# Written order on all queues, eight pairs by seven products, and whole rows of scores, in a packed attention with a gated MLP

## The chip, the cores and the metric

The kernel runs on one core of a Trainium2 chip. The metric is the device time of one execution in microseconds; three runs of the kernel before gave 707.8, 708.59 and 708.6 us, median 708.59. The profile is of one more execution, whose span from the first to the last instruction is 707.7 us.

The names of the engines are those of the profile: PE is TensorE's matmuls, PEld its weight loads, DVE is VectorE, ACT is ScalarE, POOL is GpSimd, SP is SyncE, whose queue issues nearly all DMAs.

## What is computed

```python
# q, k, v: 8 batches x 8 heads x 576 rows x 64;  p: 8 x 8 x 32 x 64;  fp32
def sm_attn(qq, kk, vv):
    s = scale * (qq @ kk.T)
    a = exp(s - max(s)); a = a / (sum(a) + 1e-9)
    return a @ vv
p_packed = sm_attn(p, k, v)               # 32 packed rows per head
out = sm_attn(q, p_packed, p_packed)      # 576 x 64 per head
x = out with the heads side by side       # 4608 x 512
h = x @ w_in                              # w_in 512 x 2048, float64 on input
g = h * clip(h + 3, 0, 6) / 6
return g @ w_out                          # w_out 2048 x 512, float64 on input
```

## The kernel before

**Stages.** The packed rows are multiplied with w_in first ("m", 256 x 2048 for a batch, 32 packed rows of 8 heads), so the first product of a batch is m against the second softmax a: 256 deep, in two groups g. The 2048 columns of w_in are 16 blocks f of 128. For each f, `first_product` (L929) makes h for some rows of the batch; `gate_into` (L940 on ACT, L941 on DVE) makes h * min(relu(h + 3), 6); `split` (L946 on ACT, L947 on DVE or POOL) writes that as a hi and a lo part in fp32r; and `product` (L969) multiplies them with w_out, which is kept as hi and lo too. Every product is therefore three matmuls: hi by hi, hi by lo, lo by hi.

**Rows.** A batch has 576 rows, 4 x 128 and a boundary of 64. They are done in two halves c of 2 x 128 rows. One half of each batch is wide: its first product also covers the 64 boundary rows (320 columns instead of 256), whose gated values `keep_edge` (L965, POOL) puts into `bnd`. The boundary rows of two batches make one block of 128 rows for the second product. Before the change, those of batches 0 and 1 and of 2 and 3 are multiplied plainly in batches 1 and 3 (`edge_parts`, `edge_product`); those of 4 to 7 are multiplied in one pass in batch 7 (`moe_edges`), with rows of batches 4 and 5 kept in DRAM meanwhile (`e_kept`).

**Seven products.** Two blocks f, two blocks of 128 rows and two halves of 256 output columns make a 2 x 2 by 2 x 2 product, which `pair_product` does with seven products of 256 columns instead of eight. The right factors are blocks of w_out and four combinations of them, T1 to T4; T3 takes a block's place, and T1, T2, T4 lie in tiles wt in the places of w_in's chunks 1 to 3. `combine` makes them once, in batch 1. The left factors are the gated blocks A11 to A22 and sums S1 to S4 (L1241, L1249, L1254 on DVE), split in tiles ge, gf and ga. The sums pile up in four PSUM banks A, B, C, D, and at the end of a half `pair_product` puts C and D together (L1134 on ACT, L1136 on POOL, L1139 on DVE) and `single_product` adds A and B (L1153) and stores the rows (L1156). PAIRS = 6 of the 8 pairs are done like this; the other four f are singles, plain products of 512 columns, at the end of each half. Batch 0 has all f plain, batch 1 its first half plain and 4 pairs in its second. Of the six pairs' T blocks four lie in SBUF at a time; `fetch_t` (L1105) brings pairs 0 or 4 and 1 or 5 back from DRAM (768 KB each), twice in each half.

**Attention of the next batch** runs beside the MLP of this one. Scores, in 32-column tiles of the array, come from `each_head` (L350) into PSUM, in the steady part half a row (288 columns) at a time, through banks that the accumulators leave free; e is transposed (L440), multiplied with v (L470), and the second scores and softmax follow. The quarters of m come from `u_m`, also L350, 512 columns each, with w_in's chunk fetched from DRAM into one place, w_in0 (1 MB each, L1428).

**What sets the order.** Batch 0 and the start of batch 1's attention are written out by hand: PLAN is a list of names, and each name takes one step of a generator; all of PE, DVE, ACT, POOL and SP follow that list. `ENGINES` says which engine does a step that several can do. From batch 1 on, the planner of the tile framework orders the instructions by its own estimates, within limits: `second` puts products one pair behind their first products, `behind_gates` holds the attention's steps behind gates, and STAGES, LATE, TURN and FETCHES say at which f which step may start.

**The start.** The inputs of batch 0 come in rows of four (1 KB runs) and a remainder of 64 rows by itself (`long_rows`, `rest_rows`, `load_rows`), so scores and transposes of batch 0 have a long and a short part (L678, L694, L720, L731, L803). Tiles of w_in and w_out, 512 KB in float64 each, are loaded in between and narrowed to fp32 by ACT, DVE and POOL (L199, L203).

Of the kernel before, what the change touches and what calls it, by code (L numbers as in the profile page):

```python
# [20 lines left out]


STAGES = (((0, 1), (6, 2), (19, 2)), ((0, 1), (10, 2), (19, 1)))


LATE = (3, 2, 1, 2, 1)
PAIRS = 6
FIRST_PAIRS = 4
TURN = (
    (5, 5, 6, 6, 7, 7, 7), (7, 8, 8, 9, 9, 9, 10), (10, 10, 11, 11, 12, 12, 12), (13, 13, 13, 14, 14, 15, 15),  # L30
    (27, 27, 28, 28, 28, 29, 29), (29, 29, 30, 30, 30, 31, 31),
)
FETCHES = (((5, 1), (7, 0)), ((5, 4), (7, 5)))

PLAN = """
in in in in lo0 lo2 in in k0 in p li0 k1 in p k0 k2 k1 kr k2 in s0 kr b2 s0 b0 k3 s0 b2 li1 s0 warm b2 s0 in
k3 b2 in b0 s1 s0 li2 q1 b2 e0 q1 c0 s1 b2 e0 q0 c0 li3 s0 s1 v0 q0 s0 s1 s1 v0 b0 lp s1 b0 e1 a0 v0 c1 qr
v0 e1 c1 s1 a0 z0 qr b0 s1 a0 z0 b0 v1 a0 z0a a1 z0a upper a1 z0a lo1 q2 v1 li4 a1 q3 q2 z0a a1 v1 q3 v1 z0a  # L40
z1 z1 li7 a2 m0 z1a a2 m1 a2 z1a a2 lo3 a3 z1b z0a lk0 a3 z1b z1b z0a z1b z0a z1a z0a z1b lo5 z1a b1 li6 z1a
z1b m0 z1b b1 z1a z1a z1b z0a a4 z1a m0 li5 z1b z0a warm a3 z1b z0a m1 m0 z1b a7 lk2 z1a h0 m0 z1a m1 b1 a7
z1a b1 b3 h0 b3 lo4 b3 a3 warm r0 m1 a4 r0 b3 m2 lo8 tp h1 r0 m1 a7 y0 b1 h1 r0 m2 lo6 a4 x0 b1 r1 a4 x0 m2
m2 a6 r1 x0 a6 m2 h2 a7 tk0 r1 h2 y1 a5 lk3 r1 a5 x0 y1 a5 x1 r2 a6 a5 b5 x1 r2 b3 x1 tk2 r2 y0 h3 a6 b4 r2
lk1 h3 b4 b5 m4 x1 b3 r3 b4 li8 b5 m4 b4 li10 r3 x2 li9 m4 m4 x2 lo7 r3 m4 b5 below h4 b4 tk3 y3 b6 h4 b4 y3
lq1 y2 b6 x2 r3 b5 x2 b6 r4 tk1 x3 b6 b8 r4 x3 a8 b5 S a8 x3 a8 r4 y4 a8 S S S S x3 b8 y4 h5 a10 li11 r4 a10
lo9 h5 a10 a9 b8 lq3 x4 b8 r5 x4 b6 r5 S x4 y2 a10 r5 tq1 h6 lo10 b8 r5 lq2 h6 y5 a9 y5 S x4 a9 r6 b8 x5 a9
S b7 S x5 r6 a11 x5 li12 S a11 a11 h7 b6 r6 a11 S h7 r6 x5 b9 r7 li13 m8 S lv b7 b7 x6 r7 y6 b7 m8 x6 y7 r7
m8 m8 x6 y6 S tq3 r7 b7 h8 S b10 m8 lq0 x6 b10 b7 y7 a12 h8 b10 b9 b9 x7 b10 tq2 r8 lo12 x7 S lw0 r8 x7 b9
a13 E h9 r8 S h9 y8 a13 a13 y8 lo11 r8 E a13 r9 x7 b10 x8 r9 E E tq0 b9 h10 a12 b9 lw1 E h10 S a12 y9 b12  # L50
b10 a12 x8 r10 x8 r9 li14 r10 E b12 x8 y9 li15 E r10 b12 h11 r9 b11 h11 r10 b11 b11 V r11 b11 x9 V V b12 b11
lo15 r11 T x9 a14 T a14 Z lo13 a14 b12 x9 a14 a15 Z a15 a15 x10 y11 Z a15 x9 b15 Z Z x10 r11 b11 m12 b15 x10
r11 b15 m12 b12 b15 x10 m12 m12 y10 x11 b13 m12 h12 Z y11 b15 lo14 y10 b13 Z h12 b13 x11 r12 b13 x11 Z r12
x11 Z r12 h13 b15 b14 h13 r12 b14 M b14 r13 x12 Z b14 b13 r13 Z x12 b14 Z r13 h14 Z y12 y12 h14 b13 x12 r13
r14 x12 Z r14 x13 Z r14 h15 Z y13 h15 y13 Z x13 b14 stage r15 x13 r14 y14 Z x13 r15 x14 Z r15 x14 y14 M Z
r15 x14 Z M M x15 Z x15 o0 Z x15 y15 o0 o1 M x14 Z o1 y15 x15 Z o3 o3 o2 o2
"""

ENGINES = {
# [16 lines left out]
def packed_attention_moe(  # L78
# [4 lines left out]
    v: bass.AP,  # L83
    p: bass.AP,
    w_in: bass.AP,
    w_out: bass.AP,
    out: bass.AP,
):

# [21 lines left out]
    scale = 1.0 / float(D) ** 0.5  # L111
    H2 = DM // 2
    W = 2 * P + REM
    WT = 2 * W

    const = ctx.enter_context(tc.tile_pool(name="const", bufs=1))
    mp = [ctx.enter_context(tc.tile_pool(name="mp", bufs=1))]
# [1407 lines left out]
```

## Time and profile before

| | before |
|---|---|
| median of three runs | 708.59 us (707.8 to 708.6) |
| span of the profiled execution | 707.7 us |
| PE: in flight | 684.7 us, 5924 matmuls |
| DVE busy | 544.2 us |
| ACT busy | 428.8 us |
| POOL busy | 335.9 us |
| DMA | 111 MB, 157 GB/s over the span |
| mean granted clock of TensorE | 0.990 of full speed |

Busy time of PE counts matmuls in flight, which overlap, so its share is no measure of pace. The distance between the starts of two matmuls is; the chain of waits in order of time shows it, since a run of matmuls that follow each other without a wait stands there as one piece with its length. Idle time stands beside the work that ended it.

### The profile page before, as it was taken

The numbers are of one execution on the slowest core, as the hardware profiler recorded it, in microseconds if no ns is written. First come the engines' busy times: TensorE is split into PE (matmuls) and PEld (weight loads), VectorE is DVE, ScalarE is ACT, GpSimd is POOL, SyncE is SP. The second block draws the span as 40 slices with busy tenths as digits, with TensorE's granted clock in tenths as the row PEclk, the third lists the DMA queues.
The fourth block names the chain that finished last, engine by engine and source line by source line (L and its number), as shares of the span: only waits on it lengthen the run. The fifth ranks groups of instructions, "written<-read, shape, count | busy, mean of one in ns | idle before, by whom it ended". The sixth has DMA issues, their size and how long they took to land.

```text
span 707.7 us, 16190 instructions
## 1 busy us (share of the span) xinstructions
PE 684.7 (97%) x5924; PEld 591.9 (84%) x5924; DVE 544.2 (77%) x1227; ACT 428.8 (61%) x1004; POOL 335.9 (47%) x515
## 2 busy tenths in 40 slices
PE   6599999999999999999999999999999999999997
PEld 4477877888879888899898888899888988899997
DVE  2897788788999759877788777877698778867754
ACT  5798876556566646565455655656475755565553
POOL 2475541113425456371272626474453646475552
PEclk9699999999999999999999999999999999999999
DMA  9989852955338655465554647375755644340330
GB/s 277 310 216 240 218 141 88 287 150 116 117 123 208 161 131 210 127 158 108 107 200 125 164 103 232 121 158 129 196 200 143 168 127 150 129 170 1 120 119 30
DMA packets 199679, 111.15 MB, mean 157 GB/s; under 512 B 173489, under 2 KB 185265, under 8 KB 195761
## 3 DMA queue, kind: packets, MB, share of 16 engines
q1 hardware_dynamic: 199056, 109.94, 55.8%
q8 instruction: 46, 0.75, 0.4%
q14 instruction: 33, 0.26, 0.1%
q10 hardware_dynamic: 544, 0.20, 0.1%
HBM read 92.27 MB, written 17.83 MB: 156 GB/s over the span
## 4 chain that ended last, share of the span: by engine, by line
PE 82%; DVE 7%; DMA 5%; issue 2%; SPq 1%; ACT 1%; POOL 1%; DVEq 0%; ACTq 0%; POOLq 0%
PE acc L969 48%; PE ps_hh L929 22%; PE ps L350 5%; PE ps_h L607 3%; DMA w_again<-w_kept 2%; PE ps L470 1%; SPq L294 1%; DMA room<-in_q_dram 1%; PE ps L440 1%; DMA wt<-t_kept 1%; DVE tr L555 1%; DMA p_nat<-in_p_dram 1%; DVE osb L1153 1%; PE ps L273 1%; DVE t L941 0%
## 5 line engine op out<-in xcount | busy, mean ns | idle before, releaser
L929 PE MATMUL ps_hh<-a_hi,m_hi 128*128 128x320 f32 (+1 forms) x448 | 133.5, 298 | 1.0 <-DVE t L941 0.9
L929 PE MATMUL ps_hh<-a_lo,m_hi 128*128 128x320 f32 (+1 forms) x448 | 133.0, 297 | 0.0
L929 PE MATMUL ps_hh<-a_hi,m_lo 128*128 128x320 f32 (+1 forms) x448 | 132.7, 296 | 0.0
L969 PE MATMUL acc<-wo_hi,g 128*128 128x512 f32 x304 | 109.0, 402 | 0.0
L940 ACT ACTIVATE t<-ps_hh,three 128x320 f32<-128x320 f32 (+1 forms) x148 | 73.5, 500 | 47.4 <-PE ps_hh L929 36.0
L941 DVE SCALAR_TENSOR_TENSOR t<-t,ps_hh 128x320 f32<-128x320 f32 (+1 forms) x148 | 65.7, 445 | 45.1 <-ACT t L940 44.4
L947 POOL TENSOR_TENSOR ge<-t,ge 128x256 fp32r<-128x256 f32 x76 | 60.3, 793 | 80.8 <-ACT ge L946 32.1
L929 PEld LDWEIGHTS ps_hh<-a_hi,m_hi 128*128 128x128 f32 x448 | 84.7, 189 | 7.7 <-DVE t L941 2.7
L929 PEld LDWEIGHTS ps_hh<-a_lo,m_hi 128*128 128x128 f32 x448 | 84.7, 189 | 4.8 <-issue 1.9
L929 PEld LDWEIGHTS ps_hh<-a_hi,m_lo 128*128 128x128 f32 x448 | 84.7, 189 | 1.7 <-issue 1.3
L965 POOL COPY bnd<-t 128x64 f32<-128x64 f32 x76 | 24.2, 318 | 120.0 <-DVE t L941 117.8
L969 PE MATMUL acc<-wt,ga 128*128 128x256 f32 x492 | 80.4, 284 | 0.3 <-ACT ga L946 0.2
L969 PE MATMUL acc<-wo_hi,ge 128*128 128x256 f32 x328 | 77.8, 285 | 0.0
L947 POOL TENSOR_TENSOR gf<-tb,gf 128x256 fp32r<-128x256 f32 x76 | 65.0, 855 | 17.5 <-ACT gf L946 14.9
L947 POOL TENSOR_TENSOR ga<-t,ga 128x256 fp32r<-128x256 f32 x76 | 60.8, 800 | 24.4 <-ACT ga L946 24.2
L969 PEld LDWEIGHTS acc<-wo_hi,g 128*128 128x128 f32 x304 | 56.1, 188 | 16.2 <-issue 3.0
L969 PEld LDWEIGHTS acc<-wt,ga 128*128 128x128 f32 x492 | 68.0, 190 | 1.2 <-issue 0.5
L969 PEld LDWEIGHTS acc<-wo_hi,ge 128*128 128x128 f32 x328 | 57.5, 190 | 7.0 <-issue 2.8
L969 PE MATMUL acc<-wo_lo,g 128*128 128x512 f32 x152 | 60.1, 395 | 0.0
L555 DVE STREAM_TRANSPOSE tr<-nat 128x576 f32<-128x576 f32 x56 | 42.4, 765 | 16.7 <-DMA nat<-in_q_dram 10.4
L940 ACT ACTIVATE tb<-ps_hh,three 128x256 f32<-128x256 f32 (+1 forms) x76 | 37.9, 499 | 23.0 <-PE ps_hh L929 18.6
L969 PE MATMUL acc<-wt,gf 128*128 128x256 f32 x246 | 50.1, 283 | 0.3 <-DMA wt<-t_kept 0.3
(234 smaller groups left out, 1780.5 us busy)
## 6 DMA issues: line engine op xcount, KB each, us to landing
w_again<-w_kept SPq DMA_DIRECT2D x24, 1024.0 KB, 4.8
wt<-t_kept SPq DMA_DIRECT2D x26, 768.0 KB, 5.2
out_dram<-osb SPq DMA_DIRECT2D x35, 256.0 KB, 2.4
nat<-in_k_dram SPq DMA_DIRECT2D x112, 72.0 KB, 3.2
nat<-in_q_dram SPq DMA_DIRECT2D x112, 72.0 KB, 2.7
raw_out<-in_moe_w_out_dram SPq DMA_DIRECT2D x10, 512.0 KB, 5.1
raw_in<-in_moe_w_in_dram SPq DMA_DIRECT2D x10, 512.0 KB, 5.6
w_kept<-w_in_sb SPq DMA_DIRECT2D x4, 1024.0 KB, 7.6
```

Of the source, the lines that this page charges most:

```text
L273: nc.tensor.matmul(banks[x][NPK * a:NPK * a + NPK, :n * P], state["pp"][half, NPAIR * x + a], cols[half, :, a], start=True, stop=True,)
L294: nc.sync.dma_start(out=t[r:r + 32], in_=src[b, 2 * a + h, :, 32 * c:32 * c + 32].rearrange("(t i) j -> i t j", i=32),)
L350: nc.tensor.matmul(pair[x][NPK * a:NPK * a + NPK, :n], rows[half, a], c, start=True, stop=True)
L440: nc.tensor.transpose(out=pair[x][:, c * P:(c + 1) * P], in_=e[x][:, c * P:(c + 1) * P], identity=ident)
L555: nc.vector.transpose(out=t, in_=state.pop(("nat", which, b, a)))
L607: nc.tensor.matmul(h[:, hf, :HS], mm[:, g, fs], aa[:, hf * HS:(hf + 1) * HS], start=(g == 0 and i == 0), stop=(g == NG - 1 and i == 2),)
L929: state["first"] = nc.tensor.matmul(h[:, :n], mm[:, g, fs], aa[:, t0:t0 + n], start=(g == 0 and i == 0), stop=(g == NG - 1 and i == 2),)
L940: state["relu"] = nc.scalar.activation(out=t[:, :n], in_=h, func=AF.Relu, bias=three)
L941: state["gate"] = nc.vector.scalar_tensor_tensor(out=t[:, :n], in0=t[:, :n], scalar=6.0, in1=h, op0=ALU.min, op1=ALU.mult)
L947: engine.tensor_sub(out=lo, in0=x, in1=hi.bitcast(F32))
L965: nc.gpsimd.tensor_copy(out=bnd[:, f, side * REM:side * REM + REM], in_=t[:, boff:boff + REM])
L969: nc.tensor.matmul(out, lhs[x], rhs[y], start=first and i == 0, stop=last and i == 2, skip_group_check=True)
```

## The change

The whole steady part is taken from the planner. There is a list for each batch 1 to 7 (PLANS), and every step of every engine and of SP's queue is emitted in the list's order, so first products, gates, splits, second products, fetches and the next batch's attention are interleaved by the list alone. A name with "-" is a step left from the batch before.

- All eight pairs are done by seven products, from the second half of batch 2 on; the first half of batch 2 has six pairs and four singles, batch 1 stays as it was (plain, then 4 pairs). Four of the eight pairs' T blocks lie in SBUF; pairs 6 and 7 stay, the other six go through two places, and `fetch_t` brings four of them in each half. Halves run alternately up and down through the pairs so that the last two fetched are the first two of the next half.
- The boundary rows of batches 0 to 3 become one pass by seven products in batch 3, like that of 4 to 7 in batch 7 (`half` with c = 2).
- Scores of a whole row come in one stay: 64 columns into the unused ends of the two banks of the first products, 512 columns into two banks of their own. The accumulators keep fixed banks.
- The lo parts of pairs go to POOL unless ENGINES names DVE: it does for 134 of the 392 in the halves.
- The four sums of the last pair come in an order that finishes C and D first.
- Batch 0: its inputs come in runs of six rows (1.5 KB, 96 partitions), nine loads ahead of the first weights; the remainder and its short steps are gone. PLAN is new, and so are the engines of many of its steps.

```diff
-PAIRS = 6
-FIRST_PAIRS = 4
+PLANS = (
+    """
+-m2 -m2 -m2 -m2 s00 g00 s01 -m2 lk1 g00 g00 g00 -m1 s02 g01 g01 kw -m1 -m1 g00 s00 g01 g01 g01 lk2 g02 s01 -m1
...
+        def turn_rows(x, i):
...
+            for j in range(n):
+                h, y = divmod(n * i + j, Y0)
+                src = nat["k", h // 4][:, h % 4] if x == "k" else nat["q", h // 2][:, h % 2]
+                nc.tensor.transpose(
+                    out=ps[:, j * R0:(j + 1) * R0],
+                    in_=src[:R0, 2 * y:2 * y + 2].rearrange("p c d -> p (c d)"),
+                    identity=ident[:R0, :R0],
+                )
...
+    def fetch_t(i, n):
+        nc.sync.dma_start(out=place(i, n), in_=t_kept[i])
+        yield
...
+        def pair_products(i):
+            todo = [
+                ("A", 0, "A12", "B21"), ("C", 0, "A11", "B11"), ("D", 1, "S3", "T3"), ("A", 1, "S4", "B22"),
+                ("B", 0, "A22", "T4"), ("D", 0, "S1", "T1"), ("C", 1, "S2", "T2"),
+            ]
+            if i == pairs[0]:
+                todo = [todo[k] for k in (1, 2, 0, 3, 4, 5, 6)]
+            if i == pairs[-1]:
+                todo = [todo[k] for k in (1, 6, 2, 5, 0, 3, 4)]
+            for x, at, l, r in todo:
+                fresh = x not in banks
+                stop = i == pairs[-1] and (x in "CD" or order[-1][0] == "P")
+                product(bank(x)[:, at * H2:at * H2 + H2], lhs[i][l], block(i, r), fresh, stop)
+                yield
+
+        def pair(i, turn):
+            for k in range(2):
+                made[2 * i + k] = first_product(b, 2 * i + k, t0, n, turn + k)
+                yield
+            yield from pair_products(i)
...
+    def rows_by_head(lhs, rhs):
+
+        t = [att(x) for x in range(2)]
+        for cols, to in ((slice(512, S), [h[:, 512 - REM:] for h in hh]), (slice(0, 512), t)):
+            for a in range(NPAIR - 1, -1, -1):
+                for x in (1, 0):
+                    at = slice(64 * x, 64 * x + 64)
+                    nc.tensor.matmul(
+                        to[x][NPK * a:NPK * a + NPK], lhs[at, a], rhs[a][at].rearrange("p t i -> p (t i)")[:, cols],
+                        start=True, stop=True,
+                    )
+        return t
...
+    UP, DOWN = (0, 1, 2, 3, 4, 5, 6, 7), (5, 4, 3, 2, 1, 0, 7, 6)
+    SLOTS = {0: 0, 1: 1, 2: 0, 3: 1, 4: 0, 5: 1}
...
+            n_pairs = {(1, 1): 4, (2, 0): 6}.get((b, c), 8)
+            turns = turn_of(b, c)[:n_pairs]
+            order = [("P", i) for i in turns] + [("S", f) for f in range(2 * n_pairs, NF)]
...
+            if b > 1:
+                for i in turns[4:6] if n_pairs == 6 else turns[2:6]:
+                    chains[f"f{c}{i}"] = fetch_t(i, SLOTS[i])
...
+        if b in (3, FOUR + 3):
+            turns = turn_of(b, 2)
+            half(chains, b, 2, [("P", i) for i in turns], [edge_rows(x) for x in (b - 2, b)])
...
+        for b, plan in enumerate(PLANS, 1):
+            chains = {"-" + name: chain for name, chain in chains.items()}
+            later_moe(chains, b)
+            if b + 1 < B:
+                later_attention(chains, b + 1)
+            for name in plan.split():
+                next(chains[name])
```

## Rows read from the trace of the kernel before

**Rows 1.** Page, part 1: PE's busy time, share of the span, instructions.
```profile
PE 684.7 (97%) x5924; PEld 591.9 (84%) x5924; DVE 544.2 (77%) x1227; ACT 428.8 (61%) x1004; POOL 335.9 (47%) x515
```

**Rows 2.** PE's waits: engine, tile, line <- awaited: us in total, times, longest.
```profile
PE ps_t L886 <- DVE m_lo L286: 5.3, 1, 5.3
...
PE ps_w L803 <- issue: 2.0, 1, 2.0
PE ps L273 <- POOL w_in_sb L203: 1.1, 1, 1.1
...
PE ps_hh L929 <- DVE tb L941: 0.2, 1, 0.2
```

**Rows 3.** Chain of waits in order of time: start us, us, what, count.
```profile
19.22 0.22 PE ps_w L731 x13
...
56.24 0.65 PE ps_w L350 x16
...
238.66 1.44 PE ps_hh L929 x12
240.10 2.52 PE acc L969 x21
...
268.11 1.02 PE ps L350 x16
...
312.93 1.76 PE ps_hh L929 x12
...
451.74 1.39 PE acc L969 x6
```

**Rows 4.** Groups of PE's instructions, shapes apart: busy us, mean ns, idle before.
```profile
L969 PE MATMUL acc<-wt,ga 128*128 128x256 f32 x492 | 80.4, 284 | 0.3 <-ACT ga L946 0.2
```

**Rows 5.** Timeline of three stretches: start us, us, engine, line, operation, idle before.
```profile
33.40 0.80 PE L607 MATMUL ps_h<-a_hi,m_hi 128*128 128x288 f32 x1
...
403.38 0.28 PE L969 MATMUL acc<-wo_lo,ge 128*128 128x256 f32 x1
403.58 0.71 PE L350 MATMUL ps<-tr,p_tr 64*32 64x288 f32 x16
...
696.75 0.60 ACT L1134 ACTIVATE osb<-acc 128x512 f32<-128x512 f32 x1 [0.27 <-PE acc L969]
...
697.43 0.73 POOL L1136 TENSOR_TENSOR osb<-osb 128x256 f32<-128x256 f32 x1 [2.81 <-ACT osb L1134]
...
703.22 1.39 DVE L1153 SCALAR_TENSOR_TENSOR osb<-acc,osb 128x512 f32<-128x512 f32 x2 [1.62 <-PE acc L969]
...
703.48 0.39 PE L969 MATMUL acc<-wo_hi,g 128*128 128x512 f32 x1
```

**Rows 6.** Windows: us, PE, PEld, DVE, ACT, POOL busy, clock, DMA share, GB/s.
```profile
0.00:33.40 33.40, 18.72 (x312) 13.20 (x313) 17.43 (x47) 20.42 (x43) 11.61 (x16) 0.83 1.01 289
30.00:34.00 4.00, 1.26 (x3) 0.84 (x3) 3.78 (x13) 3.74 (x11) 2.92 (x4) 0.50 0.88 199
310.00:390.00 80.00, 80.00 (x718) 70.06 (x718) 62.79 (x146) 45.26 (x116) 32.91 (x49) 1.00 0.50 137
```

**Rows 7.** View of tile wt, last line: whole run, then 680 to 681 us.
```profile
DMA to landing us min/median/max: 3.3/5.1/7.1
...
DMA to landing us min/median/max: 4.2/4.2/4.2
```

**Rows 8.** DVE's and POOL's groups from 110 us on: count, busy, mean ns, idle.
```profile
L1249 DVE TENSOR_TENSOR t<-t,tb 128x256 f32<-128x256 f32 x76 | 43.5, 572 | 1.5
...
L1254 DVE TENSOR_TENSOR tb<-tb,t 128x128 f32<-128x128 f32 x76 | 36.8, 484 | 1.6
...
L947 DVE TENSOR_TENSOR g<-t,g 128x256 fp32r<-128x256 f32 x72 | 30.1, 423 | 6.4 <-ACT g L946 4.7 <-PE acc L969 0.5
...
L1241 DVE TENSOR_TENSOR t<-t 128x128 f32<-128x128 f32 x76 | 24.6, 323 | 1.9
...
L947 POOL TENSOR_TENSOR gf<-tb,gf 128x256 fp32r<-128x256 f32 x76 | 65.0, 855 | 17.5 <-ACT gf L946 14.9 <-POOL ge L947 1.1 <-POOL bnd L965 0.8
```

More of the change, by code (lines that the diff above doesn't have):

```diff
@@ L342, in each_head @@
             for pair, cols in reversed(list(zip(banks, rounds))):
-                for a in (range(NPAIR - 1, -1, -1) if steady else range(NPAIR)):
+                for a in range(NPAIR):
                     for x in (1, 0):
@@ L366, in both_halves @@
             yield None
-            yield from ((hf, done[hf]) for hf in ((0, 1) if steady else (1, 0)))
+            yield from ((hf, done[hf]) for hf in (1, 0))
         else:
@@ L838, in s2 @@
             made["z", g] = [(s, z, at, mx, den, hi, lo, slice(i, i + n)) for i in range(0, T, n)]
-            next(parts)
-            yield
+            yield from products(s, g, made["pp"].rearrange("p (x h) n -> p x h n", x=2), turned["q"])
         def s2_part(g, i):
@@ L1000, in edge_product @@
-    def edge_product(acc, f, hi, lo, summed, first, last):
-        def lhs(k):
-            return [x[:, k * P:(k + 1) * P] for x in (hi, lo)]
-        if not summed:
-            for k in range(2):
-                second_product(f + k, acc, *lhs(k), first=first and k == 0, last=last and k == 1)
-            return
-        i = f // 2
-        second_product(f, acc, *lhs(0), first=first, last=False)
-        product(acc[:, :H2], lhs(1), block(i, "B21"))
-        product(acc[:, H2:], lhs(2), block(i, "B22"))
@@ L1107, in sums_of @@
-    def sums_of(pairs, rows):
-        banks, made = {}, {}
+        yield from kept_as("T4", x)
+        yield from kept_as("T3", y)
+        if i < 6:
+            whole_slot = [(t_kept[i], slot)] if n < 3 else [
+                (t_kept[i][:, k * DM:(k + 1) * DM], kept[m][:, 3].bitcast(F32).rearrange("p x m -> p (x m)"))
+                for k, m in enumerate((2, 0, 1))
+            ]
+            for dst, src in whole_slot:
+                nc.sync.dma_start(out=dst, in_=src)
+                yield
@@ new lines, in edge_again, with half @@
+    def edge_again(i):
+        t = xp.tile([P, W + P], F32, name="e_again", tag="tb")[:, :4 * REM]
+        kept["e", i] = t.rearrange("p (f n) -> p f n", f=2)
+        nc.sync.dma_start(out=t, in_=e_kept[:, 4 * REM * i:4 * REM * (i + 1)])
+        yield
+    def fetch_t(i, n):
+        nc.sync.dma_start(out=place(i, n), in_=t_kept[i])
+        yield
+    def half(chains, b, c, order, rows, n=None, t0=0, off=0, boff=0, side=None):
+        pairs = [i for kind, i in order if kind == "P"]
+        banks, lhs, made, pos = {}, {}, {}, 0
@@ new lines, in quarter @@
+    def quarter(b, n):
+        t = [att(x) for x in range(2)]
+        for a in range(NPAIR - 1, -1, -1):
+            for x in (1, 0):
+                at = slice(64 * x, 64 * x + 64)
+                nc.tensor.matmul(
+                    t[x][NPK * a:NPK * a + NPK], pps[b % 2][at, a], w_in_sb[n][at, :, a], start=True, stop=True
+                )
+        yield
+        hi, lo = m_tiles(b, n)
+        for x in range(2):
+            nc.scalar.copy(out=hi[:, x], in_=t[x])
+            yield
+            nc.vector.tensor_sub(out=lo[:, x], in0=t[x], in1=hi[:, x].bitcast(F32))
+            yield
```

1189 lines of the change are left out of this document (621 added, 568 removed), and 43 rows, old and new, of the table ENGINES.

## The prediction

> **What bounds the kernel now.** I read the busy times first: TensorE (PE) has work in flight for 684.7 of 707.7 us [rows 1]. That alone does not say that it works at its pace, so next I looked at what it waits for. The list of PE's waits has 14 rows; the long ones belong to the start (5.3 and 2.0 us among them), and the seven that fall after the first 33 us, from 1.1 down to 0.2 us, add up to 4.4 us in 674 [rows 2]. So in the steady part nothing but the number and the pitch of matmuls sets the time. The pitch I take from the chain of waits in order of time, where a run of matmuls stands as one piece: 21 matmuls of 256 columns in 2.52 us (0.120 each), 12 first products of 256 columns in 1.44 and of 320 in 1.76 us, six of 512 columns in 1.39 us (0.232 each) [rows 3]. The granted clock is 1.00 (the 2.4 GHz level) in the steady stretch and 0.50 (1.2 GHz) in the stretch shown of the start [rows 6]. The start is another stage: PE is busy for 18.7 of its first 33.4 us, and the first product of the first batch begins at 33.40 us [rows 5, 6].
>
> **Seven products for all pairs.** A pair of f done plainly on 2x128 rows is 2x2x3 = 12 matmuls of 512 columns, 12 x 0.232 = 2.78 us; by seven products it is 7x3 = 21 of 256 columns, 2.52 us. A pair gains 0.26 us. How many pairs change side: the 492 matmuls of ga against wt are 6 in each pair's products, so before has 82 pairs [rows 4]: 4 in batch 1, 6 in each of 12 later halves, 6 in the one boundary pass. After, the code gives 4 in batch 1, 6 in the first half of batch 2, 8 in each of 11 halves, and 8 in each of two boundary passes: 114. That is 32 more. The boundary rows of batches 0 to 3, which before are done plainly with matmuls of 512 columns, are part of it. 32 x 0.26 = **8.4 us less**, all of it on the path, since PE is the path. The first products are untouched.
> The Trainium skill ("TensorE: Matmul & The Clock Gate", Back-to-back issue gap) gives a warm gap of N/2.4 + 2.5 ns, 109 and 216 ns for these two sizes; that is an estimate by that page. By it a pair would gain 0.30 us and the whole 9.6 us. The measured pitches, 120 and 232 ns, are longer for both, and they decide.
>
> **Whole rows of scores per stay.** Before, a batch's scores come in two stays of eight 288-column matmuls, 0.65 us each [rows 3], and entering one costs 0.08: the 256-column matmul ahead of it takes 0.20 us to the next start instead of 0.12 [rows 5]. After, one stay does 64 and 512 columns. Eight of 512 take 1.02 us; eight of 32 take 0.22 [rows 3], 64 perhaps 0.28. So 2 x (0.65 + 0.08) = 1.46 us becomes 0.08 + 0.28 + 1.02 = 1.38, twice in each of six batches: **1.0 us less**. Bounds: if the 64 columns run on without a step of their own, 3 us less; if the 64 columns, which now lie in the same banks as the first products' output, make the next first product wait for the two copies and the two maxima out of there, up to 1 us more each time, 12 us more. I take the value next to the rows, because the written order puts second products behind the scores.
>
> **Written order instead of the planner's.** It adds no work. What it can take is the 4.4 us of steady idle [rows 2]; what it can add are new waits. I walked through the written lists and added PE's pitches between the end of a product and the matmul that needs what follows from it. From a pair's last first product to the first use of what its odd f gives lie 3.6 us at least and 7.7 in the median; before it was the products of the pair ahead plus two first products, 2.52 + 1.44 to 1.76 = 4.0 to 4.3, and the chain of relu, gate and split fitted in that with hardly a wait. So it mostly has more cover. A quarter of w_in has at least 7.8 us from the buffer's release to its use. I take **2.3 us less**, about half, bounds 0 and 4.4.
>
> **Fetches of the T blocks.** Six pairs now go through two places, so each half has 4 fetches (54 in all, before 26). A fetch landed after 3.3 to 7.1 us, 5.1 in the median, and 4.2 when alone near the end [rows 7]. By the same walk the time between the last use of a place and the first use of the next block is 6.1 to 12.5 us in the halves, but 5.0 to 6.8 in the eight of the boundary passes, where no first products lie between. Sum of what is missing: 0.2 us if all land in 5.1, 4.6 us at 6.0, 19 us at 7.1. SP issues in order, so a fetch that waits for its place also holds the k, q, v and w_in loads behind it; these have several us to spare. Batch 7's pass has no next batch's loads and should be near 4.2; batch 3's is not. I take **1.0 us more**, bounds 0.2 and 19.
>
> **The elementwise engines.** A pair needs three VectorE (DVE) sums (0.572, 0.484 and 0.323) and no longer two lo parts (0.423 each): +0.53 us [rows 8], four pairs a batch, +2.1. The table of engines moves 134 of the pairs' 392 lo parts from GpSimd (POOL), 0.855 us [rows 8], to DVE, +8.7 us a batch. DVE has 62.8 us of work in 80 [rows 6], 60.8 in a batch of 77.5. That makes 71.6 us in a batch in which PE has 16 x 2.52 + 8 x (1.44 + 1.76) + about 9.7 of attention = 75.6: 95% at most, since DVE's neighbours overlap a little. It stays hidden, at no cost to the sum; it is the thinnest cover, and what it costs when gone is the second rival.
>
> **The start.** The inputs of batch 0 now come in nine long loads ahead of all weights. Before, weight tiles stand between them, and PE waits 2.0 us for rows of v and later 5.3 us for DVE [rows 2]. All nine are 3.6 MB, 12.6 us at 289 GB/s [rows 6]. The second group's scores should come about 3 us earlier; DVE, 3.78 busy of 4 us before the first product [rows 6], gets the z products and more copies and gives part back. The weights of f = 0 land later, behind three other tiles, near 20 us, and have 10 us. I take **2.5 us less**. Bounds: 7.3 less (both waits gone), 3 more (narrowing w_in becomes last, or the half clock lasts longer).
>
> **The end.** The last half has no single f behind which the four sums are put together. From C's last product: the copy 0.60, GpSimd's add 0.73 [rows 5], three DVE sums near 0.4, A's row sum 0.70 and half of B's 0.4, 3.7 us, of which five products of 0.36 cover 1.8. Before, DVE ends 0.7 us behind PE (703.22 + 1.39 against 703.48 + 0.39) [rows 5]. **1.2 us more**, bounds 0 and 2.
>
> **Sum.** 707.7 - 8.4 - 1.0 - 2.3 + 1.0 - 2.5 + 1.2 = 695.7 us for a profiled execution. The median of the runs is 0.9 us above that execution's span, so **696.6 us**, 1.7% faster. Its own range from the likely bounds is 690 to 702.
>
> **Rivals.**
> *T fetches land late.* Twice the fetches beside the same loads; before, fetches taken two at a time reached 7.1 us. For it: the passes' windows of 5.4 us. Against: most windows are above 7. From about 6 us landing on, each tenth costs; at 7.1 us 19 us, hence 700 to 715. Chance 0.14, a third of it ending within or above the old time.
> *DVE becomes the bound* (the slower side). It decides when DVE's work in a batch passes PE's 75.6 us, 4 us above my sum. Its price: a 256-column sum of pairs has a mean of 0.572 us, a lo part of the same size in the singles 0.423 [rows 8], so such instructions do get slower in company; if the 24 moved lo parts a batch took twice 0.42 among the pairs, DVE would need 82 us, 6.4 over PE in each of five batches, 697 + 32 = about 729, and 713 where half of that comes true. For it: 95% is high. Against: each moved part takes GpSimd work away, and so the contention itself. Chance 0.10.
> The Trainium skill ("GPSIMD Engine Reference", the table at its head) says that GpSimd's SBUF interfaces are shared with VectorE, with contention where VectorE has two SBUF inputs. By that rule this rival is the one to fear, and the trace agrees in so far as those sums are the ones with the long means.
> *The scores' stay waits at the shared banks*: 12 x 1 us, 707. Chance 0.05.
> *The start does not gain or loses* (low clock, late weights): 699 to 702. Chance 0.07.
>
> **How the numbers follow.** Forecast 0.64. Range 688.5 to 705: it takes in the start's good end and the fetches up to 6.5 us; left out are DVE, the worse half of the fetches, and a little below. About 0.2% is what a measurement of this kernel can tell from no change. Faster: 0.64 + 0.09 (fetches) + 0.02 (banks) + 0.07 = 0.82; within 0.2%: 0.05 (0.02 and 0.03 of these two); slower: 0.10 + 0.03 = 0.13.
>
> **What would show it.** 684 of the ga-wt matmuls in place of 492, no 512-column boundary matmul, pitches unchanged; PE's steady idle near 2 us with wt as its largest row; DVE above 90% in a batch; the first first-batch product near 31 us; DVE ending 2 us behind PE at the end. Wrong would be: PE waiting on DVE's gates or sums in every batch, wt waits in the halves, or a longer pitch of 256-column matmuls where nearly all are of that size.

## The result, and the profile after

The change made the kernel slower. The median of four runs is 715.26 us (713.4 to 718.4) against 708.19 in the same series: ratio 1.011, 95% interval 1.008 to 1.014. The forecast was 696.6 with a range of 688.5 to 705. The profiled execution of the kernel after is the longest of the four; its span is 716.6 us, some 3 above that of the median.

The lines of the page that answer to [rows 1], [rows 4] and [rows 7], and those of its parts on the DMA queues and issues (packets, MB, share of 16 engines; KB each, median us to landing):

```profile
PE 680.8 (95%) x6142; PEld 602.7 (84%) x6142; DVE 588.6 (82%) x1424; ACT 431.5 (60%) x1062; POOL 327.6 (46%) x505
...
q1 hardware_dynamic: 204480, 135.76, 69.2%
...
L949 PE MATMUL acc<-wt,ga 128*128 128x256 f32 x684 | 106.2, 287 | 0.0
...
wt<-t_kept SPq DMA_DIRECT2D x54, 768.0 KB, 4.7
w_again<-w_kept SPq DMA_DIRECT2D x24, 1024.0 KB, 6.1
...
nat<-in_q_dram SPq DMA_DIRECT2D x112, 72.0 KB, 3.6
```

The change does what it says: 684 matmuls of ga against wt, and 54 fetches. PE is in flight for less time than before, 680.8 against 684.7 us, yet the whole is longer. So it waits more. Its waits, to be read beside [rows 2] (us in total, times, longest):

```profile
PE acc L949 <- DMA wt<-t_kept: 8.7, 6, 2.1
PE ps_t L424 <- POOL w_in_sb L366: 6.6, 2, 6.3
...
PE h L971 <- DVE tb L984: 1.6, 2, 0.9
```

The first row is what is new: 8.7 us for T blocks, where the kernel before has

```profile
PE acc L969 <- DMA wt<-t_kept: 0.3, 1, 0.3
```

Windows of the kernel after (us, busy time of PE, PEld, DVE, ACT and POOL, granted clock, DMA share, GB/s):

```profile
30.00:42.00 12.00, 10.33 (x75) 7.36 (x60) 10.34 (x24) 9.49 (x21) 9.87 (x8) 0.50 0.94 239
...
278.30:281.60 3.30, 3.30 (x16) 3.30 (x15) 1.70 (x4) 1.62 (x5) 0.81 (x3) 0.50 0.81 92
394.00:416.00 22.00, 19.19 (x179) 17.77 (x178) 14.96 (x43) 12.12 (x34) 6.05 (x9) 1.00 0.95 218
```

The second line is one of two stretches of the steady part at half clock (the other begins at 561.5 us); before, the clock was 1.00 there throughout. Both stand right behind a wait for T. The chain of waits in order of time shows the first of them (start, us, what):

```profile
269.18 8.65 DMA wt<-t_kept
...
277.87 2.65 PE acc L949 x12
```

A fetch lands 8.65 us after its issue, and the 12 matmuls behind it take 0.22 us each instead of 0.12. The third window is a half in which four T fetches meet the next batch's q loads: the DMA engines are 95% busy. SP's queue there (start, us that the issue held the queue, line):

```profile
394.44 0.38 SPq L1089 DMA_DIRECT2D wt<-t_kept  x1
394.91 3.13 SPq L445 DMA_DIRECT2D nat<-in_q_dram  x4
398.14 2.71 SPq L1089 DMA_DIRECT2D wt<-t_kept  x1
400.94 2.49 SPq L445 DMA_DIRECT2D nat<-in_q_dram  x4
403.53 1.70 SPq L1089 DMA_DIRECT2D wt<-t_kept  x1
```

T blocks and q loads alternate, and the T issues behind q loads hold SP for 1.7 and 2.7 us; the median of all T issues is 0.3. Why an issue takes longer there is not shown; q loads in short runs are still under way at both. The three T blocks issued here landed after 6.6, 7.6 and 6.7 us. Of all 54, the 15 issued with k or q loads still under way landed after 4.7 to 8.65 us (6.5 in the middle), the other 39 after 3.9 to 6.6 (4.5).

By stages, from the two profiled executions:

| stage | before | after | difference | forecast |
|---|---|---|---|---|
| to the first product | 33.4 | 30.7 | -2.7 | -2.5 |
| from there to the end of batch 0 | 85.6 | 89.2 | +3.6 | 0 |
| batches 1 to 7 | 584.9 | 591.4 | +6.5 | -10.7 |
| behind the last matmul | 3.8 | 5.2 | +1.4 | +1.2 |

So two stages missed: batch 0, and the steady part by 17 us. Both figures are of one execution, and these stages differ from one execution to another: in ten profiles of kernels whose instructions up to there are the same (the kernel after and nine of the runs below), batch 0 ends at 119.7 to 123.2 us, in the middle at 121.5 (after 119.95; before, in its one profile, 119.0). In six profiles with the same steady part (the kernel after, and the five runs whose edit is at the start alone), that part takes 585.9 to 591.5 us. So the steady part misses its forecast by 12 to 17 us, and batch 0 ends 1 to 4 us later than before. Three theories were set against each other: T blocks land late (theory 1); the start pays its gain back, through a late w_in and a low clock (theory 2); VectorE, with 588.6 us of work, is what is late (theory 3, the second rival of the prediction).

### The profile page after: what moved, and what is told of

The parts are those of the page before. It is cut to its first block, busy times and chain, and to the rows that moved or that the text cites. A ratio compares the mean times of both kernels' runs of the same rounds, so it can differ in the third digit from the quotient of the medians.

```text
span 716.6 us, 17067 instructions
## 1 busy us (share of the span) xinstructions
PE 680.8 (95%) x6142; PEld 602.7 (84%) x6142; DVE 588.6 (82%) x1424; ACT 431.5 (60%) x1062; POOL 327.6 (46%) x505
## 3 DMA queue, kind: packets, MB, share of 16 engines
q1 hardware_dynamic: 204480, 135.76, 69.2%
## 4 chain that ended last, share of the span: by engine, by line
PE 72%; DMA 11%; DVE 8%; ACT 2%; SPq 2%; issue 2%; POOL 2%; DVEq 0%; POOLq 0%; ACTq 0%
PE acc L949 39%; PE h L971 21%; DMA w_again<-w_kept 4%; PE ps_h L699 3%; PE at L1396 3%; DMA wt<-t_kept 3%; DMA nat<-in_q_dram 2%; SPq L445 2%; PE at L1368 1%; PE at L1294 1%; DVE tr L689 1%; DMA p_nat<-in_p_dram 1%; POOL ga L993 1%; PE ps_t L760 1%; DMA e_again<-e_kept 1%
## 5 line engine op out<-in xcount | busy, mean ns | idle before, releaser
L971 PE MATMUL h<-a_hi,m_hi 128*128 128x320 f32 (+1 forms) x448 | 136.3, 304 | 1.9 <-DVE tb L984 1.6
L971 PE MATMUL h<-a_lo,m_hi 128*128 128x320 f32 (+1 forms) x448 | 133.2, 297 | 0.4 <-DVE a_lo L666 0.4
L971 PE MATMUL h<-a_hi,m_lo 128*128 128x320 f32 (+1 forms) x448 | 133.0, 297 | 0.0
L982 ACT ACTIVATE t<-h,three 128x320 f32<-128x320 f32 (+1 forms) x126 | 63.0, 501 | 66.2 <-PE h L971 40.7
L971 PEld LDWEIGHTS h<-a_hi,m_hi 128*128 128x128 f32 x448 | 85.5, 191 | 14.9 <-DVE t L984 4.2
L993 POOL TENSOR_TENSOR ga<-t,ga 128x256 fp32r<-128x256 f32 (+1 forms) x80 | 62.8, 785 | 59.3 <-ACT ga L991 46.9
L971 PEld LDWEIGHTS h<-a_lo,m_hi 128*128 128x128 f32 x448 | 85.5, 191 | 1.4 <-DVE a_lo L666 0.6
L971 PEld LDWEIGHTS h<-a_hi,m_lo 128*128 128x128 f32 x448 | 85.3, 190 | 0.0
L949 PE MATMUL acc<-wo_lo,ge 128*128 128x256 f32 x228 | 63.9, 280 | 0.0
L949 PE MATMUL acc<-wo_hi,gf 128*128 128x256 f32 x228 | 60.8, 289 | 0.0
## 6 DMA issues: line engine op xcount, KB each, us to landing
wt<-t_kept SPq DMA_DIRECT2D x54, 768.0 KB, 4.7
```

Of the source, the lines that this page charges most:

```text
L949: nc.tensor.matmul(out, lhs[x], rhs[y], start=first and i == 0, stop=last and i == 2, skip_group_check=True)
L971: nc.tensor.matmul(h, mm[:, g, fs], aa[:, t0:t0 + n], start=(g == 0 and i == 0), stop=(g == NG - 1 and i == 2),)
L982: nc.scalar.activation(out=t[:, :n], in_=h, func=AF.Relu, bias=three)
L993: on(name, engine).tensor_sub(out=lo, in0=x, in1=hi.bitcast(F32))
```

## Experiments on the steady part

Each is an edit of the kernel after. The time of the kernel before was 708.0 to 708.2 us in every series.

**A sixteenth of each fetch.**

```diff
-        nc.sync.dma_start(out=place(i, n), in_=t_kept[i])
+        nc.sync.dma_start(out=place(i, n)[:, :96], in_=t_kept[i][:, :96])
```

> The changed kernel, but each of its 54 fetches of T blocks brings only 96 of the 1536 words of a row (49 KB instead of 786 KB); the rest of the fetch is left out, so later pairs multiply with old T blocks. All other work is that of the changed kernel. Theory 1 (T fetches land late, behind the loads that stand ahead of them in SP's queue, and TensorE's clock falls behind two of the long waits): the wt waits go (about 10 us) and the two half-clock stretches at 278 and 561 us with them (about 3 us): the time after batch 0 falls from 591.4 to 578-580, in all 702-704. Theory 3 (VectorE, 82% busy, is what is late): its work is as it was, so 712 or more.

702.2 us, 0.992 of before (0.989 to 0.995). No wt row is left among PE's waits, no half clock in the steady part, and batches 1 to 7 take 575.3 us. Late T blocks cost 13.0 us, of which only 8.7 stand in the row of waits (5.3 to 6.4 in the five other profiles with the same steady part). The rest was not split by an experiment; in the kernel after, the clock behind two of the waits makes some 3 us of it, and other loads in the queue are late too: VectorE's wait for q loads is 18.0 us there, 6.3 here. VectorE's work is unchanged (589.6 us, after 588.6), so theory 3 falls here.

**Half of each fetch** (768 of 1536 words).

> e1_short_fetch with half of each T fetch (768 of 1536 words of a row); the other half of the fetch is left out. Theory 1 in the form that the 16 DMA engines' throughput decides (T block and q loads of a pair take 4.7 us of transfer against 4.0-4.3 us of TensorE): half a T block takes 1.7 us less, the transfers keep up, and all wt waits go: 701-704, as with a sixteenth. If instead each fetch is late by a wait in the queue that does not depend on its size, about half of the 13 us stays: 707-711.

704.8 us (0.994 to 0.997 of before), just above the expected range; landing 3.4 us in the median, no wt wait, batches 1 to 7 in 575.1. Half the bytes cure 10.5 of the 13 us, where a wait that does not depend on size would have left half: it is a matter of throughput.

**Fetches first.** The fetch names move up in PLANS, for example

```diff
-... lq1 ... f02 tq1 ...
+... f02 ... lq1 ... tq1 ...
```

> The changed kernel with 47 of its 54 T fetches moved up in the written order to right behind the product that reads their place last, and so ahead of the k, q and w_in loads that stood before them; nothing else. Theory 1: the wt waits of the halves go, as a fetch alone lands in 4.4 us and the windows there are 6.1 us or more; those of the boundary passes (windows of 5.0 to 6.8) may stay with up to 2 us: 703-707. If what makes fetches late is not their place in the queue but the loads that run beside them on the same DMA engines, the waits stay and it is 712 or more. Theory 3: 714-717.

768.0 us, far from all of these. PE's waits, and VectorE's:

```profile
PE at L1396 <- DMA w_again<-w_kept: 16.1, 3, 8.3
PE h L971 <- DVE tb L984: 11.1, 2, 6.6
...
DVE tr L689 <- DMA nat<-in_q_dram: 34.6, 8, 7.4
```

The wt wait is gone (0.3 us). But SP, in order, stands at a fetch until its place is free (127.1 us in all, up to 7.3 at once; 93.3 and 5.5 in the kernel after), and the q and w_in loads behind it come late; VectorE, in order too, stands at the transpose of q, and the gates behind that are late for PE. The loads have nothing to spare. The order in the kernel after is a trade between the two, and far the better one.

**Fetches on ScalarE's queue**, with the new places and with the old.

```diff
-        nc.sync.dma_start(out=place(i, n), in_=t_kept[i])
+        nc.scalar.dma_start(out=place(i, n), in_=t_kept[i])
```

> The changed kernel with all 54 T fetches issued by ScalarE's queue, written right behind the product that reads their place last (the places of e2_fetch_first); SP keeps every other load, and no longer waits for a place to come free. Theory 1, with the reading of e2_fetch_first that its loss came from the k, q and w_in loads behind the waiting fetches in SP's queue: both go, 702-706. Rival: a fetch that shares the 16 DMA engines with the loads lands as late as one queued behind them: wt waits of 5 us or more stay, 711 or more. Second rival: ScalarE, waiting in its queue for a place, makes the high parts of the next gates late: waits of TensorE for ACT, above 712.

> The changed kernel with all 54 T fetches issued by ScalarE's queue, at the places in the written order that they have in the changed kernel; nothing else. Theory 1: a fetch no longer stands behind the loads, but ScalarE issues it at the place of its name, for many only just ahead of the first use in the written order: 703-712, better than the changed kernel only where ScalarE runs some us ahead of TensorE.

780.2 and 792.8 us. ACT's longest row of waits in the first, PE's in the second:

```profile
ACT gf L991 <- PE acc L949: 34.6, 18, 3.8
...
PE acc L949 <- DMA wt<-t_kept: 56.0, 21, 5.6
```

In the first the second rival came true: ACT waits for a place to come free, with the next pairs' splits behind it. In the second ACT reaches the fetch's name only when the block is already due. What the transfers would do on a queue that nobody else uses stays open: no engine is free to hold it. The Trainium skill ("DMA: Bandwidth & Descriptors", Issuing engines are not separate DMA queues) says that DMAs of several engines interleave on the same 16 DMA engines. No run here separates that from a queue of its own: the median landing of T is 4.4 and 4.8 us in these two kernels against 4.7.

**Low parts back to POOL.** 132 entries `"e404": "D"` and the like leave ENGINES.

> The changed kernel with 132 of its subtractions that make low parts (gates e, f and h of the pairs) put back from VectorE to GpSimd; nothing else. Theory 3 (VectorE's load is what costs the time after batch 0): VectorE's busy time falls by some 60 us of 589 and the time to 711 or less. Theory 1: the waits for wt are as they were, and the time is 714 or more, more where GpSimd's slower subtraction is late for its product.

722.6 us, 1.019 of before (1.015 to 1.023), 7 us more than the kernel after. Its busy times and two rows of PE's waits:

```profile
PE 684.9 (95%) x6142; PEld 605.3 (84%) x6142; DVE 573.6 (79%) x1292; ACT 432.4 (60%) x1062; POOL 413.3 (57%) x637
...
PE acc L931 <- DMA wt<-t_kept: 7.2, 5, 2.6
...
PE acc L931 <- POOL ge L975: 2.5, 3, 1.0
```

VectorE loses only 15 us of work (60 expected), POOL gains 86, the wt wait stays and POOL's splits become late. Some 55 us of subtractions did leave VectorE, but its other sums take longer beside a busier POOL: the 128-column sum of two gates 0.417 us instead of 0.341. So VectorE's work hardly fell, and this run is a weak test of theory 3; what refutes it is that the first two experiments took the loss away with that work unchanged.

**Long runs for k and q.** Each load takes 32 runs of 2304 bytes instead of 576 of 128.

```diff
-                    out=t[r:r + 32],
-                    in_=src[b, 2 * a + h, :, 32 * c:32 * c + 32].rearrange("(t i) j -> i t j", i=32),
+                    out=t[r:r + 32].rearrange("i t j -> i (t j)"),
+                    in_=src[b, 2 * a + h].rearrange("(i t) j -> i (t j)", i=32)[:, 32 * T * c:32 * T * (c + 1)],
```

> The changed kernel with the k and q loads of batches 1 to 7 in runs of 2304 bytes instead of 128, the same 72 KB in each DMA and the same number of DMAs; the values land in another order, so the scores of these batches are of other numbers. If the short runs are what fills the DMA engines beside the T fetches: the wt waits go, 702-706. If the bytes alone decide (q's 288 KB at the pace of a T block would be 1.2 us of the 4.7): 711-716.

705.3 us, 0.996 of before (0.994 to 0.997): with whole fetches and all loads. Queue, window and wait of this kernel:

```profile
q1 hardware_dynamic: 82624, 135.76, 62.3%
...
394.00:416.00 22.00, 21.16 (x262) 20.49 (x268) 16.94 (x50) 12.79 (x36) 5.32 (x9) 1.00 0.69 204
...
PE acc L949 <- DMA wt<-t_kept: 2.2, 5, 0.8
```

The same 135.76 MB in 82624 packets instead of 204480. This takes 10 of the 13 us away. So neither T's bytes nor q's alone make the fetches late, but T blocks beside loads in short runs. The Trainium skill ("DMA: Bandwidth & Descriptors", Why small descriptors are slow) gives a packet from HBM a fixed overhead beside its bytes; the runs agree in so far as the same bytes keep the queue busy for 62.3% of the span instead of 69.2%. The four T blocks of this half, which in the kernel after land 4.5 to 5.0 us apart, land 3.6 to 3.7 us apart (395.94, 399.55, 403.11 and 406.80 us). VectorE's wait for q loads falls with it, from 18.0 us to 1.7.

**Three parts of a fetch**, in the order of use.

```diff
-        nc.sync.dma_start(out=place(i, n), in_=t_kept[i])
+        to = place(i, n)
+        for k in (2, 0, 1):
+            cols = slice(k * DM, (k + 1) * DM)
+            nc.sync.dma_start(out=to[:, cols], in_=t_kept[i][:, cols])
```

> The changed kernel with each T fetch as three DMAs of 256 KB, in the order in which a pair's products use T4, T1 and T2, 0.36 us apart; nothing is left out. Theory 1: the block needed first lands some 2 us before the last of the three, and what is needed last is needed 0.7 us later, so each late fetch costs 0.7 us or more less: of 13 us 4-8 go, 708-712. Rival: three issues in place of one hold SP's queue longer, and the k and q loads land late instead: 715 or more.

710.35 us: 5 of the 13 us, as theory 1 has it, with 2.1 us of wt waits left (8.7 before the edit).

**Fewer fetches.** First, two pairs of four halves became plain singles:

> The changed kernel with 8 of its 114 pairs put back to plain products: the third and fourth pair of the first half of batches 3 to 6, where the q loads of the next batch run; their 8 T fetches go, and the 8 that stay there get windows of some 16 us instead of 6-9. Theory 1 (there the transfers need more time for a pair, T block and q loads together, than TensorE): the wt waits at 306, 404, 482 and 559 us (7.1 us) and the half clock at 561 (1.5 us) go, and 8 pairs cost 0.26 us more each (2.1 us): 715.3 - 6.5, so 707-710. If the wait only moves to the fetches that stay: 714 or more.

708.9 us, in the range. (It multiplies with T3 where the plain product needs the block that T3 replaced; the time is that of plain pairs.) With nothing left out, by eight products:

```diff
+                (("A", 0, 1, "B21"), ("B", 0, 1, "B21")), (("A", 0, 0, "B11"),), (("B", 0, 0, "B11"),),
+                (("A", 1, 0, "T3"),), (("B", 1, 0, "T3"),), (("A", 1, 2, "B22"),), (("B", 1, 2, "B22"),),
```

> The changed kernel with nine of its 114 pairs (the third and fourth of the first half of batches 3 to 6, the fourth of the second half of batch 2) by eight products that need only the blocks that stay in place (the upper columns from T3 and B22, with the sum of the two gates), so nine of the 54 T fetches go; in batch 2 the fetch that is left for that place moves to where the dropped one stood. Nothing of the computation is left out. Theory 1: the wt waits at 276, 306, 404, 482 and 559 us and both half-clock stretches after batch 0 go (12 us at most, 8.9 of them waits), and eight products cost 0.36 us more than seven for nine pairs (3.2 us): 706-710. Rival: VectorE, which makes one sum less but is in order, is late elsewhere, 712 or more.

710.8 us (1.003 to 1.007 of before); no wt row, no half clock in the steady part. Just above its range: the waits go, and the nine eighth products, 3.2 us by the estimate above, come.

## Experiments on the start

Four starts of matmuls in the first batch (start, us, line, operation), the first of them from the kernel before: the first second product in either kernel, and ahead of it the first products of f = 0 and f = 1 after.

```profile
40.46 0.40 PE L969 MATMUL acc<-wo_hi,gh 128*128 128x512 f32 x1
```

```profile
30.71 0.61 PE L699 MATMUL ps_h<-a_hi,m_hi 128*128 128x288 f32 x1 [0.40 <-ACT m_hi L435]
...
36.66 0.58 PE L699 MATMUL ps_h<-a_hi,m_hi 128*128 128x288 f32 x1 [0.74 <-ACT m_hi L435]
...
40.84 0.79 PE L949 MATMUL acc<-wo_hi,gh 128*128 128x512 f32 x1
```

The lead of 2.7 us is gone ten microseconds later: the first second product starts at 40.84, before at 40.46.

**w_in of f = 0 before that of f = 2** (names exchanged in PLAN).

> The changed kernel with the w_in chunks of f = 0 and f = 2 exchanged at the start, in their load as in their four narrowing steps; nothing else. Theory 2 (TensorE's 6.3 us of waiting for the narrowed chunk of f = 0 sets the first product, and the half clock of the 12 us behind it follows from that idle time): that chunk lands 4 us earlier, the first product starts at 27-28.5 instead of 30.7, and the half clock ends earlier: 710-712. Rival: the low part of a, which VectorE finishes at 30.9, is late just behind it: the first product's second matmul waits for it, and the time stays within 714-716.

716.3 us, close to the rival's result, though by another path than it named. PE's waits:

```profile
PE ps_t L424 <- POOL w_in_sb L366: 4.3, 2, 4.0
PE ps_h L699 <- ACT m_hi L435: 3.6, 2, 2.9
```

2.3 us less for w_in, 2.5 more for ACT's copy of m right behind it. The first product comes at 34.4 us here, but this profile has the late start told of at the end; so has that of the low parts on POOL, whose start is that of the kernel after and whose first product comes at 34.7. Against that one, too, it is 2.5 us less for w_in and 2.5 more for the copy.

**Dummy matmuls in the idle time**, 40 and then 12.

```diff
-... li0 q4 z1 z0a ...
+... li0 q4 z1 warm warm warm ... z0a ...
```

> The changed kernel with 40 matmuls of 256 columns on zeros, whose results nobody reads, written on TensorE behind the last scores of the first batch, where it otherwise waits 6.3 us for the narrowed w_in; nothing else. Theory 2 (the first products run at half clock because TensorE was idle ahead of them, which in the changed kernel costs 6-8 us of batch 0 against 1.5 before): the half clock ends 5-10 us earlier, batch 0 falls from 89 to 83-86 and the time to 709-712. If the clock does not follow this: 714-717, or later by up to 3 us where the dummies themselves run at half clock.

> e5_warm with 12 matmuls of 256 columns on zeros instead of 40 (each took 0.44 us there, 17.5 us in all, so 5.3 us here, less than the idle 6.3): the first product is not delayed. If the idle time ahead of it kept the clock at half, batch 0 falls to 83-86 and the time to 709-712; if the gaps behind it do, as e5_warm suggests, the half clock still lasts 6 us or more behind the first product and the time is 712-716.

727.7 and 714.8 us. The 40 took 17.5 us instead of some 5 and pushed the first product to 41.85: mis-sized. The 12 fit, and the clock shows what the idle time had to do with it:

```profile
26.00:30.00 4.00, 2.66 (x27) 1.78 (x25) 3.97 (x13) 4.00 (x9) 1.89 (x2) 1.00 1.04 241
30.00:31.50 1.50, 1.31 (x6) 0.94 (x6) 1.47 (x6) 1.44 (x4) 1.45 (x2) 1.00 0.53 118
31.60:41.80 10.20, 8.42 (x54) 6.02 (x54) 8.59 (x17) 7.77 (x17) 8.45 (x7) 0.50 1.04 278
```

Full clock up to the first products, half clock during them, for 10 us. In the kernel after the clock falls earlier, in the idle time:

```profile
24.00:26.00 2.00, 0.00 (x0) 0.00 (x0) 2.00 (x5) 1.57 (x4) 1.56 (x2) 0.91 1.10 376
26.00:30.00 4.00, 0.38 (x16) 0.23 (x16) 3.93 (x11) 4.00 (x9) 2.37 (x2) 0.50 1.07 250
```

So the idle time does lower the clock, but with it filled the clock falls all the same, a little later. Theory 2's mechanism, idle time ahead as the cause of the slow first products, is wrong as it stands.

**The first product behind m of f = 1**, so that it runs without gaps; and **the gaps filled** with eight more dummies.

```diff
-... b0 h0 z1b h0 li5 m1 tk2 b3 b3 r0 r0 ...
+... b0 z1b li5 m1 tk2 b3 b3 h0 h0 r0 r0 ...
```

> The changed kernel with TensorE's two steps of the first batch's first product (f = 0) moved in the written order to behind the step that makes m for f = 1; nothing else. Reading of e5_warm: the half clock behind the first product does not come from the idle time ahead of it but from the gaps between the first products (0.2 to 0.7 us, for a, m and w_in). Then the first product starts at 35-36 instead of 30.7, runs without gaps, the half clock ends within 4 us of it instead of 9-12, batch 0 takes 84-86 instead of 89, and the time stays within 714-717. If the half clock again lasts 9 us or more behind the first product, the gaps are not its cause, and the time is 718-721.

> e11_warm12 with eight more matmuls of 256 columns on zeros, three behind each half of the first product and two behind the step that makes m for f = 1, where TensorE waits 0.2 to 0.7 us (up to 1.4 us at full clock). If the gaps between the first products hold the clock at half: no half clock behind the first product, or one that ends by 36; batch 0 falls from 89-90 to 84-86; 708-712. If the half clock still lasts to 40 or later, its cause is another one, and the time is 714-718.

716.6 and 714.7 us. Windows of the first, then of the second:

```profile
35.40:38.40 3.00, 3.00 (x19) 2.87 (x12) 0.00 (x0) 0.00 (x0) 0.72 (x1) 0.50 1.06 214
38.50:42.00 3.50, 1.79 (x13) 1.63 (x12) 2.39 (x6) 3.37 (x8) 0.99 (x1) 1.00 0.91 290
```

```profile
31.00:34.30 3.30, 3.30 (x11) 2.73 (x11) 3.12 (x8) 2.08 (x5) 2.51 (x2) 0.50 1.04 328
34.40:42.00 7.60, 7.48 (x68) 5.80 (x67) 5.67 (x11) 6.20 (x13) 5.33 (x6) 1.00 1.06 254
```

In both the half clock now ends within 3 to 5 us of the first product, so the gaps did hold it. Yet the time hardly moves: in the second kernel the first second product starts at 40.16 (after 40.84) and batch 0 ends at 119.8 (after 120.0). The product of f = 1 needs m of f = 1, and that the narrowed w_in, for which PE waits until 35.2 us in the kernel after and 34.8 in the first of these two. In the second the dummies themselves are in the way: the first line is of the kernel after, the others are of the second of these two.

```profile
35.24 0.68 PE L424 MATMUL ps_t<-w_in_sb,pp 64*32 64x128 f32 x16 [0.29 <-POOL w_in_sb L366]
```

```profile
34.96 1.46 PE L913 MATMUL ps_t<-pps 128*128 128x256 f32 x6
36.34 0.45 PE L425 MATMUL ps_t<-w_in_sb,pp 64*32 64x128 f32 x16
```

m of f = 1 starts 1.1 us later, behind six dummies, and from there to the first second product it takes 3.82 us instead of 5.60. So the full clock is worth 1.8 us on this path, and the dummies use up 1.1 of them. What it would be worth without dummies is not shown.

**Together.** The eight products with the filled gaps, and then with three-part fetches too:

> The edits of e14_eight_products and e15_no_gap together. If the two causes are separate, their gains add: 715.3 - 7 - 5 = 703, 700-706, below the kernel before (708).

> e16_both with the three-part fetches of e17_three_parts. e16_both has 1.5 us of wt waits left in its profile; these go, 707-709. If it is 705 or less, late fetches cost it more than its waits show; if above 710, the two edits are in each other's way.

709.7 (1.001 to 1.004 of before) and 710.25 us (1.001 to 1.004). The filled gaps add some 1 us (710.8 to 709.7, with intervals that overlap), not 5; and the two cures of late fetches do not add. In the last kernel 0.2 us of wt waits are left, so what remains there is not T waits. Fetches on ScalarE with 40 dummies (the edits of the two sections together) gave 793.2, the sum of both losses (12.4 and 65.0 us):

> The edits of e5_warm and e6_fetch_act together. If theory 1 and theory 2 name separate stretches, the gains add: what e6_fetch_act gains after batch 0 and what e5_warm gains in batch 0, 696-702, below the kernel before.

No version without a part left out or changed beats the kernel before.

## Why the prediction was wrong, point by point

- **Seven products, -8.4:** right. Behind batch 0 there are 636 more matmuls of 256 columns and 366 fewer of 512, at pitches that did not change (0.120 and 0.232 us): 8.6 less.
- **Scores in one stay, -1.0:** more than forecast. The stay takes 1.13 us, with the same 0.09 to enter it, against twice 0.65 + 0.09:

```profile
395.19 0.34 PE L1294 MATMUL h<-tr,p_tr 64*32 64x64 f32 x16
395.32 1.06 PE L1294 MATMUL at<-tr,p_tr 64*32 64x512 f32 x16
396.32 0.62 PE L949 MATMUL acc<-wt,ga 128*128 128x256 f32 x3
```

  The 64 columns take 0.13 us, not 0.28: the first bound, 3 us less in the twelve stays, was the value. Without late T blocks the steady part takes 575.1 to 575.3 us against 584.9, 9.6 to 9.8 less, where these two terms make 11.6. Of the 2 us between, 1.0 is one more quarter of m that comes behind the end of batch 0; the rest stays open. The gain is there; it is lost again.
- **Written order, -2.3:** 0.4 to 0.7 at most. Distances between the starts of matmuls of the full array that are over 0.2 us above their median add up, from 125 us on, to 4.3 us before and to 3.6 to 3.9 in the two kernels with short fetches. The bound of 0 was near the value.
- **T fetches, +1.0: the step that failed.** It cost 13.0 us. The median landing was better than assumed, 4.7 against 5.1 (a view that counts eight stores too; the 26 fetches alone took 5.2), and the bound of 19 us held it; the fault lies in one landing time for all fetches. I compared windows with a median and took the boundary passes for the thin place. The late ones are in the halves, where the window is longer, some 7 us for the block that PE waits for at 404 us: there each T block goes with a name of q in four loads of short runs, and the transfers of the pair take longer than the pair. From one landing of T to the next it was 4.5 to 5.0 us (401.05, 405.74, 410.25 and 415.25 us), and PE needs 2.52 + 1.44 to 1.76 = 4.0 to 4.3. The first of these four lands when it is needed, the second makes PE wait 1.9 us, the third has 2 us to spare and the fourth 0.5. Neither the median landing nor the mean DMA share of 0.50 [rows 6] can show this; it takes a sum for this stretch, of a T block and four q loads against one pair, and the prediction made none. The wait list alone tells 8.7 of the 13.
- **"These have several us to spare"** of the loads behind a waiting fetch: wrong. With the fetches first, VectorE waits 34.6 us for q and PE 16.1 us for w_in.
- **VectorE, no cost:** right, with more room than forecast. From 110 to 700 us it has 498.3 us of work in 590, 84%, not 95%. What the prediction held against its rival is borne out: the three sums of a pair take 0.482, 0.341 and 0.347 us, 1.17 in all (1.38 before), and 0.493, 0.417 and 0.389, 1.30, with the low parts put back to POOL. The rival had a chance of 0.10 and fell with the short fetches.
- **Start, -2.5:** the second step that failed. The first product came 2.7 us earlier, as forecast; the forecast took this for the whole. The supply of m for f = 1, and the half clock behind it, took it back before the first second product, and batch 0 ends 0.9 later in this profile, 2.5 later in the middle of the ten with this start. Both lie among the bounds ("narrowing w_in becomes last, or the half clock lasts longer", 3 more), and both causes named there were at work.
- **End, +1.2:** right, +1.4. VectorE's last two sums end at 713.18, two microseconds behind PE's 711.4:

```profile
712.17 1.01 DVE L1193 SCALAR_TENSOR_TENSOR osb<-acc,osb 128x512 f32<-128x512 f32 x2
```

- **The sum.** 696.6 with the three gains of the steady part at 9.7 together as measured instead of 11.7, T at 13.0 instead of 1.0, the start at +0.9 to +2.5 instead of -2.5 and the end at 1.4 instead of 1.2 is 714.2 to 715.8; measured 715.3. The rival "T fetches land late" was the case, given 0.14 and 700 to 715, with the wrong place.

## What to carry to other kernels

Where a change adds transfers, sum all transfers of a stretch (with the length of their runs) against the time of the engine that uses them, stretch by stretch; a median landing time says nothing of the stretch in which they meet. An in-order DMA queue has no free places: what is moved ahead in it takes the lateness from one load and gives it to another. And an earlier start of one product is worth what is left of it at the next thing that has to be supplied. A stage read from one profile is known only to its spread, here 3.5 us for the end of batch 0.

## What the runs showed of the hardware that was not expected

- Of the kernel after's four waits of TensorE of 1.7 to 2.1 us in the steady part, two (ending at 277.9 and 561.5 us) were followed by a stretch at half clock, which adds about 1.5 us to the wait; the other two (ending at 405.8 and 484.4 us) were not. In other profiles with the same steady part the stretch lies elsewhere (403.6 us with 12 dummies, 406.4 us with 20), and with the first product behind m of f = 1 there is none.
- The same bytes in 2.5 times fewer packets took the DMA engines' share in the window from 394 to 416 us from 0.95 to 0.69 (over the whole span, from 69.2% to 62.3%), and 10 us from the whole.
- An issue of a DMA in whose queue many short runs stand takes up to 3.8 us of SP's time instead of 0.3.
- VectorE's sums take longer beside a busier GpSimd: with 132 low parts put back (POOL's busy time from 327.6 to 413.3 us) the 128-column sum of two gates went from 0.341 to 0.417 us.
- The start differs from execution to execution: in the profile of the kernel with low parts on POOL, whose start is the same, the same scores take 1.21 us instead of 0.72, and the first product comes at 34.7 instead of 30.7 us. The trace's records of the granted clock begin, at full, at 12.0 us in the kernel after and at 23.5 in that one (the windows show 1.00 also where there is no record yet), so TensorE's other clock level, 1.2 GHz, up to there is the likely cause. The first line is of the kernel after, the second of that one:

```profile
14.35 0.72 PE L788 MATMUL ps_w<-room 64*32 64x288 f32 x16
```

```profile
15.15 1.21 PE L770 MATMUL ps_w<-room 64*32 64x288 f32 x16
```

What stays open: why batch 0 takes 78.8 to 81.4 us from its first second product on in the kernels with the new list (78.6 in the one profile before); and what one would gain by loads of k and q in long runs that still arrive in the order which the transposes need.
